# A fused attention and feed-forward kernel on one core: the written-out order of batches 2 to 7 is planned anew with longer planned DMA times

## The chip, the core and the metric

The kernel runs on one core of one Trainium2 chip. A core has a matrix engine (TensorE, PE in the profile), a vector engine (VectorE, DVE), a scalar engine (ScalarE, ACT), a general engine (GpSimd, POOL) and a sync engine (SP) that computes nothing and issues DMAs. Each engine works through its own list of instructions in order and stops at the first one whose inputs are not ready. DMAs are issued by SP, ACT or POOL and run beside the engines. The metric is the device time of one execution in microseconds (us); the median of several runs is compared.

## The reference

```python
scores = scale * np.matmul(q, k_all.transpose(0, 1, 3, 2))   # k_all: 16 beacon rows, then k
scores = np.where(causal, -1000000000.0, scores)             # the beacon columns are never masked
scores = scores - scores.max(-1, keepdims=True)
a = np.exp(scores)
a /= a.sum(-1, keepdims=True) + 1e-09
attn = np.matmul(a, v_all)
x = attn.transpose(0, 2, 1, 3).reshape(B * S, H * D)
h = x @ w_in
g = np.where(h > 0.0, h, np.exp(np.minimum(h, 0.0)) - 1.0)
out = g @ w_out
```

There are 8 batches of 8 heads, 576 tokens and 64 elements a head. `x` has 4608 rows of 512; `w_in` is 512 x 2048, `w_out` 2048 x 512. Inputs and output are float32, the products run on 16-bit types.

## The kernel before

**Attention** is done by pairs of heads, four pairs to a batch; pair 13 is the second pair of batch 3. For each pair the scores are made transposed (keys on the partitions) in two steps, `do_SC` on units (0, 1) and then on units (2, 3). Each step fills both PSUM buffers called `sc`; ScalarE takes the exponential of one unit at a time (`do_exp`) and so frees one buffer, and GpSimd zeroes the masked triangle (`do_mask`). Then the product with v follows (`do_AV`, line 473) in two pieces, (0,) with 6 matmuls and (1, 2) with 24, and VectorE divides by the sum of the row (`do_norm`).

**The feed-forward part** runs on 11 tiles of rows (three small ones and eight of 512). For each 512-row tile, 16 steps `do_mm1` (M1, line 529, four matmuls each) are followed by the exponential on ScalarE (`do_e`, line 536), a clamp on GpSimd (`do_clamp`, line 540) and a join on VectorE (`do_join`, line 549) that leaves the 16-bit activation `gt`. Then come 16 quarters `do_mm2` (M2, line 563, four matmuls each), four to a block of 128 rows, a copy out of PSUM (`do_osb`) and a store. M1 5,13 is step 13 of tile 5; M2 5,0,3 is the last quarter of the first row block of tile 5. M1, M2 and AV share four PSUM buffers called `ff`. A buffer of M1 comes back after the join, one of AV after the division.

**Loads.** In batches 0 to 2 k and q are turned by TensorE. From batch 3 (`PE_B = 3`) each batch has five loads of k (issued by SP), five of q (ACT) and five of v, all in runs of 256 bytes; a cast to bfloat16 on DVE or POOL (`cast_tok`, line 346; the strings `TOK` say which, "0" is DVE, first three letters k, last three q); and ten transposing DMAs from SP (`turn_tok`, line 353). From batch 2 the finished x rows are also turned by DMA from SP (`turn_x`, line 359, five to a batch); the first M1 of a tile waits for them.

**The order is written out by a planner.** `Plan` holds every piece of work with an engine, a sort key, a planned duration, its dependencies and the buffers that it takes and gives. `Plan.run` plays the plan through, engine by engine, smallest key first among what is ready, and emits the instructions in the order that comes out. A planned duration is nothing but a number in this play: it changes no transfer, only the order. DMAs are pieces of work on one planned "DMA" engine. The keys come from `place(b, a)`, which is `32 * (b - 1) + 8 * a + SHIFT[b]` for batch b, and from `PACES` and `LAG` for the feed-forward tiles.

When the instructions are emitted, the DMAs of SP and ACT together get eight completion semaphores in turn, and each DMA also waits until the one eight places before it has landed.

Of the kernel before, what the change touches and what calls it, by code (L numbers as in the profile page):

```python
# [138 lines left out]
def kernel(  # L139
# [122 lines left out]
    with tc.tile_pool(name="psum", bufs=1, space=bass.MemoryType.PSUM) as psum:  # L262
# [15 lines left out]
        add = plan.add  # L278
# [295 lines left out]

        SHIFT = [-8.8, -12.16, 3.82, 4.72, 5.51, 10.18, 13.79, 3.06]
        AT = [-49.72, -1.57, -0.78, 0.0, 0.42, 1.22, 1.53, -12.56]
        AT0 = [[-47.18, -49.17, -39.96, -41.23], [-43.3, -38.3, -37.64, -35.42], [-44.55, -19.83, -27.66, -35.41]]
        PACES = [(-18.35, 2.5, 7.99, 12.09), (-6.14, 3.4, 55.13, 1.74), (-8.68, 1.33, 24.3, 1.89), (37.46, 1.31, 15.04, 2.29), (66.83, 1.23, 21.13, 2.7), (104.32, 2.11, 33.83, 1.91)]  # L580
        W_AFTER = [[-52.45, -48.57, -122.34, -273.93], [16.05, 17.94, 11.68, 32.16]]
        DMA_AT = [-282.17, -172.71, 307.5]
        TOK = ("011110", "111001", "110011", "011001", "101101")
        ON_POOL = "11110000"
        X_ON_ACT = "00"
        LAG = 10.75
        URGE = -104.22
        Q_ON_ACT = "01101011"
        FIRST = (
            "q2 v0 k2 q1 v6 v9 k1 q3 k3 b1 v8 q6 q4 v1 q5 v7 v3 v2 k4 q7 k5 v5 v4 k7 k6 ").split()  # L590
        ON_ACT = "01"
        V_ON_ACT = "10011111"

        def place(b, a):
            return 32 * (b - 1) + 8 * a + SHIFT[b]

# [32 lines left out]
        def plan_v(b):  # L629
            for jc in range(NKC):  # L630
                key = load_key(f"v{NKC * b + jc}", place(b - 1, 1.8 + 0.4 * jc))
                on, eng = QUEUES[V_ON_ACT[b] == "1"]
                got = load(key, 1.22 if b < 3 else 1.3, partial(load_v, b, jc, eng), take=["vst"], issue=1.2 if jc == 0 else 0.6, units=8, on=on,
                           deps=v_issue[b - 1] if b > 1 else ())
                v_issue.setdefault(b, []).append(issues[on][-1])
                v_cast[b, jc] = add(
                    "DVE", place(b, -0.7 + 0.16 * jc), 0.56, partial(cast_v, b, jc),
                    deps=[got] + last_AV.get(b - 2, []), give=["vst"])
# [7 lines left out]
        turned, last_SC, turns, readers = {}, {}, [], {}  # L646
# [3 lines left out]
        def plan_tok(b):  # L650
            turned[b] = []
            for is_k in (True, False):
                for c in range(0, NKC, 2):
                    m = min(2, NKC - c)
                    i = (0 if is_k else 0.5) + c // 2
                    on, eng = QUEUES[ON_ACT[not is_k] == "1"]
                    gots = [load(place(b, 0) - 30 + i + 0.01 * j, 1.3, partial(load_tok, b, is_k, c + j, eng), units=8, on=on,
                                 take=["st"] if j == 0 else [], issue=1.2 if is_k and c + j == 0 else 0.65) for j in range(m)]
                    on_dve = TOK[b - PE_B][3 * (not is_k) + c // 2] == "0"
                    cast = add("DVE" if on_dve else "POOL", place(b, DMA_AT[0]) + i, 0.36 * m if on_dve else 0.53 * m,  # L660
                               partial(cast_tok, b, is_k, c, m, nc.vector if on_dve else nc.gpsimd),
                               deps=gots, take=["sb"], give=["st"])
                    for j in range(m):
                        s = add("SP", place(b, DMA_AT[1]) + i, 1.25, partial(turn_tok, b, is_k, c + j),
                                deps=[cast] + last_SC.get(b - 2, []), take=ring4)
                        turned[b].append(add("DMA", place(b, DMA_AT[1]) + i, 0.65, None, deps=[s],
                                             give=ring4 + (["sb"] if j == m - 1 else []), lat=1.0, parts=8))

        def plan_T2(n, key):
# [28 lines left out]
        def plan_pair(n):  # L698
            b, hp = divmod(n, HP)
            at = lambda a: place(b, hp + a)  # L700
            key = AT0[0][hp] - 4 if b == 0 else at(AT[1])
            ready = plan_T2(n, key) if b == 0 else plan_T(n, key) if b < PE_B else turned[b]
            masked = {}
            SC = None
            steps = [((0,), AT0[0][hp]), ((1, 2), AT0[1][hp]), ((3,), AT0[2][hp])] if b == 0 else \
                [((0, 1), at(AT[2])), ((2, 3), at(AT[3]))]
            for units, key in steps:
                SC = add(
                    "PE", key, sum(0.00024 * 2 * CUT.width[u] + 0.02 for u in units), partial(do_SC, n, units),
                    deps=ready + [SC], take=["sc"] * len(units), mode=1, lat=0.19)  # L710
                last_kq[n] = SC
                last_SC.setdefault(b, []).append(SC)
                first_SC.setdefault(n, SC)
                for u in units:
                    w = CUT.width[u]
                    x = add("ACT", key + 0.16, 0.14 + 0.00166 * w, partial(do_exp, n, u), deps=[SC],
                            take=["et"], give=["sc"])
                    masked[u] = [x]
                    for jc, q0, w in CUT.units[u]:
                        dw = min(w, P * jc + P - NB - q0, kc_sz[jc])  # L720
                        if dw > 0:
                            masked[u].append(add(
                                "POOL", key + 0.8, 0.2 + 0.0008 * 2 * dw, partial(do_mask, n, u, jc, q0, dw), deps=[x]))
                            if b < 2:
                                marks.append(masked[u][-1])
            normed = []
            for r, groups in enumerate([(0,), (1,), (2,)] if b == 0 else [(0,), (1, 2)]):
                key = AT0[r][hp] + 2.4 if b == 0 else at(AT[4 + r])
                us = [u for g in groups for u in CUT.of_range[g]]
                blks = blocks_of(groups)  # L730
                AV = add(
                    "PE", key, 0.0304 * 2 * sum(BLOCKS[i][2] for i in blks), partial(do_AV, n, groups),
                    deps=[o for u in us for o in masked[u]] + [v_cast[b, jc] for jc in range(BLOCKS[blks[-1]][2])],
                    take=["ff", "av"], give=["et"] * len(us), mode=0, lat=0.19)
                last_AV.setdefault(b, []).append(AV)
                normed.append(add(
                    "DVE", key - URGE, 0.32 + 0.148 * len(blks), partial(do_norm, n, groups),
                    deps=[AV, last_xT.get(n - 2 * HP)] + last_X.get(b - 2, []), give=["ff", "av"]))
                if b >= XB:
                    for blk in blks:  # L740
                        part.setdefault(blk, []).append(normed[-1])
                    if hp == HP - 1:
                        for blk in blks:
                            s = add("SP", at(AT[7]), 1.25, partial(turn_x, b, blk), deps=part.pop(blk), take=ring4)
                            turns.append((b, s))
                            done = add("DMA", at(AT[7]), 0.65, None, deps=[s], give=ring4, lat=1.0, parts=8)
                            last_X.setdefault(b, []).append(done)
                            for g, (lo, hi) in enumerate(CUT.ranges):
                                if lo <= BLOCKS[blk][0] < hi:
                                    scaled.update({(b * HP + p, g): done for p in range(HP)})  # L750
                    continue
                if b and r == 0:
                    continue
                if b:
                    groups, key = (0, 1, 2), at(AT[6])
                blks = blocks_of(groups)
                X = last_xT[n] = add(
                    "PE", key, sum(0.0025 + BLOCKS[i][1] / 2400 for i in blks) + 0.02, partial(do_xT, n, groups),
                    deps=normed, take=["ff"], mode=0, lat=0.19)
                w = sum(BLOCKS[i][1] for i in blks)  # L760
                normed = []
                on_act = X_ON_ACT[b] == "1"
                done = add("ACT" if on_act else "DVE", key - URGE, 0.17 + 0.00104 * w if on_act else 0.15 + w / 1920,
                           partial(do_xcopy, n, groups, nc.scalar if on_act else nc.vector), deps=[X], give=["ff"])
                for g in groups:
                    scaled[n, g] = done
# [107 lines left out]
```

## Time and profile before

| what | value |
|---|---|
| median of 3 runs | 361.16 us (360.14 to 361.88) |
| the profiled execution | 358.78 us |
| its span, first to last instruction | 356.9 us |
| PE busy | 344.9 us (97%) |
| DVE, ACT, POOL busy | 57%, 55%, 52% |
| granted TensorE clock | 1.0 of full speed |

The page of the profile gives the busy time of each engine; "the waits" list who was idle for whom; "the timeline" lists instructions in order of time, merged where equal ones follow each other, and in brackets the idle time of the engine before it and the engine or DMA that ended it. "ACTq" and "SPq" rows are DMAs being issued. "xN" at the end of a row is the number of instructions.

### The profile page before, as it was taken

What the parts mean: (1) busy time and instruction counts of PE and PEld (TensorE: products, weight loads), DVE (VectorE), ACT (ScalarE), POOL (GpSimd) and SP (SyncE); (2) the same over time, 40 slices, a digit from 0 to 9 for tenths busy, and PEclk for the clock granted to TensorE, in tenths of its full rate; (3) what the DMA queues carried; (4) which work ended last, traced back from release to release, by engine and by line L of the source; (5) the groups of instructions that cost most, each with busy time, mean ns of one, the idle gap of its engine ahead of it and who ended that gap; (6) DMA issues with size and microseconds to landing.
All of it is one profiled execution on the core that took longest, in us unless ns stands there. A gap on an engine that the chain in (4) does not pass through costs nothing.

```text
span 356.9 us, 8475 instructions
## 1 busy us (share of the span) xinstructions
PE 344.9 (97%) x3299; PEld 195.0 (55%) x3299; DVE 204.6 (57%) x421; ACT 194.6 (55%) x289; POOL 185.3 (52%) x360
## 2 busy tenths in 40 slices
PE   8998999999998999999999999999999999999996
PEld 5667887545454445545576664555555444444444
DVE  1477797565763647556856565566555545554321
ACT  2576887567554656675666547657664243433200
POOL 5487776557733664567557546555453344334200
PEclk9999999999999999999999999999999999999999
DMA  7999995799999978899999799997301311000022
GB/s 204 256 283 229 195 240 106 222 212 153 165 217 148 201 149 178 146 232 172 167 209 166 174 152 190 182 183 143 69 31 44 83 53 37 29 29 32 29 83 95
DMA packets 139480, 52.55 MB, mean 147 GB/s; under 512 B 127536, under 2 KB 131888, under 8 KB 139440
## 3 DMA queue, kind: packets, MB, share of 16 engines
q1 hardware_dynamic: 82640, 34.34, 45.7%
q10 hardware_dynamic: 52576, 13.47, 21.3%
q0 software_dynamic: 4224, 4.19, 7.0%
q8 instruction: 26, 0.43, 0.5%
q14 instruction: 14, 0.11, 0.1%
HBM read 37.22 MB, written 9.44 MB: 131 GB/s over the span
## 4 chain that ended last, share of the span: by engine, by line
PE 83%; DMA 7%; DVE 3%; POOL 3%; issue 1%; ACT 1%; SPq 1%; ACTq 0%; POOLq 0%
PE hps L529 33%; PE ops L563 33%; PE av L473 7%; PE sc L439 7%; DMA w_in<-in_moe_w_in_dram 3%; DMA st<-in_k_dram 2%; POOL et L454 2%; PE spare L274 2%; DMA kT<-st 1%; DVE gt L549 1%; DMA st<-in_beacon_k_dram 1%; ACT et L448 1%; PE tr L388 1%; POOL e L540 1%; DVE x L489 0%
## 5 line engine op out<-in xcount | busy, mean ns | idle before, releaser
L529 PE MATMUL hps<-xT,w_in 128*128 128x512 f16 (+2 forms) x768 | 141.5, 326 | 3.3 <-DMA w_in<-in_moe_w_in_dram 1.2
L563 PE MATMUL ops<-w_out,gt 128*128 128x512 f16 (+1 forms) x592 | 143.9, 374 | 0.0
L549 DVE SCALAR_TENSOR_TENSOR gt<-e,hps 128x512 f16<-128x512 f32 x144 | 97.4, 684 | 69.9 <-POOL e L540 69.6
L540 POOL TENSOR_SCALAR e<-e 128x512 f32<-128x512 f32 x144 | 89.1, 621 | 89.6 <-ACT e L536 87.6
L536 ACT ACTIVATE e<-hps 128x512 f32<-128x512 f32 x144 | 85.7, 600 | 86.7 <-PE hps L529 79.2
L448 ACT ACTIVATE et<-sc 128x768 f16<-128x768 f32 (+3 forms) x128 | 104.4, 863 | 38.4 <-PE sc L439 35.3
L529 PEld LDWEIGHTS <-w_in 128*128 128x128 f16 x768 | 67.0, 98 | 56.5 <-issue 3.4
L454 POOL TENSOR_SCALAR_AFFINE_SELECT et<-et 128x256 f16<-128x256 f16 (+2 forms) x160 | 62.0, 412 | 46.5 <-ACT et L448 43.5
L563 PEld LDWEIGHTS <-gt 128*128 128x128 f16 x592 | 54.2, 98 | 55.9 <-issue 1.7
L473 PEld LDWEIGHTS <-et 128*128 128x128 f16 (+1 forms) x960 | 36.5, 97 | 15.4 <-issue 4.1
L569 DVE COPY osb<-ops 128x512 f32<-128x512 f32 (+1 forms) x37 | 25.0, 675 | 34.4 <-PE ops L563 34.3
L473 PE MATMUL av<-v,et 128*128 128x65 f16 (+1 forms) x960 | 40.2, 193 | 2.7 <-POOL et L454 1.4
L439 PE MATMUL sc<-qT,kT 64*128 64x80 bf16 (+3 forms) x704 | 35.0, 228 | 0.0
L489 DVE TENSOR_TENSOR x<-av,rl 128x256 f16<-128x256 f32 (+2 forms) x68 | 32.0, 471 | 2.3
L439 PEld LDWEIGHTS <-kT 64*128 64x128 bf16 x704 | 20.6, 95 | 20.9 <-issue 19.3
L488 DVE RECIPROCAL rl<-av 128x4 f32<-128x4 f32 (+2 forms) x68 | 12.4, 182 | 23.5 <-PE av L473 23.1
L373 DVE CAST v<-vst 128x512 f16<-128x512 f32 (+1 forms) x40 | 21.5, 543 | 4.0 <-DMA vst<-in_v_dram 3.8
L274 PE MATMUL spare<-ones 128*128 128x256 bf16 x115 | 20.4, 300 | 1.7 <-DVE ones L812 1.3
L346 POOL CAST st<-st 128x1024 bf16<-128x1024 f32 (+2 forms) x19 | 16.2, 854 | 6.3 <-DMA st<-in_k_dram 3.4
L274 PEld LDWEIGHTS <-ones 128*128 128x128 bf16 x115 | 11.1, 107 | 6.7 <-issue 2.3
L323 POOL CAST st<-st 128x1152 bf16<-128x1152 f32 x8 | 9.1, 1142 | 5.7 <-DMA st<-in_q_dram 3.8
L346 DVE CAST st<-st 128x1024 bf16<-128x1024 f32 (+2 forms) x11 | 8.4, 762 | 1.6 <-DMA st<-in_q_dram 0.8
(35 smaller groups left out, 67.6 us busy)
## 6 DMA issues: line engine op xcount, KB each, us to landing
out_dram<-osb SPq DMA_DIRECT2D x35, 256.0 KB, 2.7
st<-in_q_dram ACTq DMA_DIRECT2D x20, 256.0 KB, 4.4
vst<-in_v_dram ACTq DMA_DIRECT2D x18, 256.0 KB, 4.5
st<-in_k_dram SPq DMA_DIRECT2D x15, 256.0 KB, 4.9
st<-in_k_dram SPq DMA_DIRECT2D x12, 288.0 KB, 7.2
st<-in_q_dram SPq DMA_DIRECT2D x11, 288.0 KB, 6.9
w_in<-in_moe_w_in_dram POOLq DMA_DIRECT2D x4, 512.0 KB, 14.2
w_out<-in_moe_w_out_dram POOLq DMA_DIRECT2D x4, 512.0 KB, 20.1
```

The costliest lines, as they stand in the source:

```text
L274: nc.tensor.matmul(out=spare[:, 0:2 * P], lhsT=ones[:, 0:P], rhs=ones, start=True, stop=True)
L439: nc.tensor.matmul(out=sc[:, h, o:o + w], lhsT=kT[D * h:D * h + D, P * jc:P * jc + P], rhs=qT[D * h:D * h + D, q0:q0 + w], start=True, sto ...
L448: nc.scalar.activation(out=et[:, :, 0:w], in_=scs[n, u][:, :, 0:w], func=AFT.Exp, bias=0.0, scale=float(1.0 / (D ** 0.5)))
L454: nc.gpsimd.affine_select(out=et[:, :, c0:c0 + dw], in_=et[:, :, c0:c0 + dw], compare_op=ALU.is_ge, fill=fill0, base=q0 + NB - P * jc, pat ...
L473: nc.tensor.matmul(out=av[:, c:c + D + 1], lhsT=ets[n, CUT.unit_of[jc, at]][0:m, h, col:col + P], rhs=v16[0:m, jc, 2 * hp + h, 0:D + 1], s ...
L489: nc.vector.tensor_tensor(out=x16s[b % 2][:, blks[0]:blks[0] + nb, P * hp:P * hp + P].rearrange("q i (h d) -> q i h d", d=D), in0=av[:, :, ...
L529: nc.tensor.matmul(out=hps[:, o:o + z - a], lhsT=w_in16[:, cc, P * fc:P * fc + P], rhs=xT[cc][:, a % RING:a % RING + z - a], start=(cc == ...
L536: nc.scalar.activation(out=e, in_=hpss[tt, i], func=AFT.Exp, bias=0.0, scale=1.0)
L540: nc.gpsimd.tensor_scalar(out=e, in0=e, scalar1=1.0, scalar2=0.0, op0=ALU.min, op1=ALU.max)
L549: nc.vector.scalar_tensor_tensor(out=gt, in0=es[tt, i], scalar=1.0, in1=hpss[tt, i], op0=ALU.subtract, op1=ALU.max)
L563: nc.tensor.matmul(out=opss[tt, t4][:, cols], lhsT=gts[tt, fc][:, P * t4:P * (t4 + 1)], rhs=w_out16[:, fc, cols], start=(fc == 0), stop=(f ...
L569: nc.vector.tensor_copy(out=osb[:, slice(*cols)], in_=opss[tt, t4][:, slice(*cols)])
```

## The change

Planned durations: a load of 256-byte runs goes from 1.3 to 1.45 us for k and q of batches 3 to 7 and for v of those batches, and a transposing DMA from 0.65 to 0.75 us. The keys of the later batches, the two last own paces of the feed-forward tiles and the offset of those behind (`LAG`) are other numbers. `TOK` moves casts: 18 of the 30 casts of batches 3 to 7 are on DVE, where there were 11. The last letter of `V_ON_ACT` lets SP and not ACT issue the v loads of batch 7. Nothing else differs; the same matmuls, activations and DMAs are emitted, in another order.

```diff
-        SHIFT = [-8.8, -12.16, 3.82, 4.72, 5.51, 10.18, 13.79, 3.06]
+        SHIFT = [-8.8, -12.16, 3.82, 7.68, 7.37, 15.72, 15.25, 20.7]
...
-        PACES = [(-18.35, 2.5, 7.99, 12.09), (-6.14, 3.4, 55.13, 1.74), (-8.68, 1.33, 24.3, 1.89), (37.46, 1.31, 15.04, 2.29), (66.83, 1.23, 21.13, 2.7), (104.32, 2.11, 33.83, 1.91)]
+        PACES = [(-18.35, 2.5, 7.99, 12.09), (-6.14, 3.4, 55.13, 1.74), (-8.68, 1.33, 24.3, 1.89), (37.46, 1.31, 15.04, 2.29), (75.69, 1.42, 8.27, 3.74), (111.87, 2.41, 34.18, 1.87)]
...
-        DMA_AT = [-282.17, -172.71, 307.5]
-        TOK = ("011110", "111001", "110011", "011001", "101101")
+        DMA_AT = [-284.54, -157.9, 350.32]
+        TOK = ("001110", "110000", "010101", "111000", "001000")
...
-        LAG = 10.75
+        LAG = 17.42
...
-        V_ON_ACT = "10011111"
+        V_ON_ACT = "10011110"
...
-                got = load(key, 1.22 if b < 3 else 1.3, partial(load_v, b, jc, eng), take=["vst"], issue=1.2 if jc == 0 else 0.6, units=8, on=on,
+                got = load(key, 1.22 if b < 3 else 1.45, partial(load_v, b, jc, eng), take=["vst"], issue=1.2 if jc == 0 else 0.6, units=8, on=on,
...
-                    gots = [load(place(b, 0) - 30 + i + 0.01 * j, 1.3, partial(load_tok, b, is_k, c + j, eng), units=8, on=on,
+                    gots = [load(place(b, 0) - 30 + i + 0.01 * j, 1.45, partial(load_tok, b, is_k, c + j, eng), units=8, on=on,
...
-                        turned[b].append(add("DMA", place(b, DMA_AT[1]) + i, 0.65, None, deps=[s],
+                        turned[b].append(add("DMA", place(b, DMA_AT[1]) + i, 0.75, None, deps=[s],
...
-                            done = add("DMA", at(AT[7]), 0.65, None, deps=[s], give=ring4, lat=1.0, parts=8)
+                            done = add("DMA", at(AT[7]), 0.75, None, deps=[s], give=ring4, lat=1.0, parts=8)
```

## The prediction

> **What bounds the kernel now.** I read the page's head first, then PE's waits, the busy time by stretches, the timeline around each gap of PE, and last the groups and the DMA issues.
>
> ```profile
> span 356.9 us, 8475 instructions
> PE 344.9 (97%) x3299; PEld 195.0 (55%) x3299; DVE 204.6 (57%) x421; ACT 194.6 (55%) x289; POOL 185.3 (52%) x360
> ...
> PE av L473 <- POOL et L454: 1.4, 1, 1.4
> PE av L473 <- DVE gt L549: 1.1, 2, 0.6
> PE hps L529 <- DVE gt L549: 0.9, 2, 0.7
> PE hps L529 <- DVE x L489: 0.8, 1, 0.8
> PE hps L529 <- DVE v L373: 0.3, 1, 0.3
> ...
> 86.00:257.00 171.00, 166.17 (x1676) 90.52 (x1675) 103.04 (x205) 105.29 (x153) 96.98 (x190) 1.00 0.97 173
> ```
>
> TensorE is the bound, at the full clock. The orders of the two kernels on PE agree up to 86 us of the trace; in the stretch from there to 257 us PE is busy for 166.2 of 171 us (the first two numbers of the last row), idle for 4.8, and the five waits of PE shown, all of them in that stretch, sum to 4.5 us. The same matmuls are issued before and after, with the same number of changes between scores and other products, so nothing but these 4.5 us can be won there. After 257 us PE has none of these waits, though the last AVs still stand there, and from about 280 us on there is feed-forward work alone.
>
> ```profile
> 332.66 20.92 PE L563 MATMUL ops<-w_out,gt 128*128 128x512 f16 x112
> ```
>
> Before, this last run of M2 has no M1 in it; after, 18 quarters of M2 (15.6 us) stand behind the last M1, so the end stays as it is: nothing there is counted.
>
> Below, a "distance" is PE's own work between two points of the written order, by these rows: 0.86 us for four matmuls of M1 or M2, 0.49 for a score step of 8 matmuls (108.00 to 108.49), 0.74 for an AV of 24, and the same for the others.
>
> ```profile
> 95.15 0.34 PE L473 MATMUL av<-v,et 128*128 128x65 f16 x6 [0.58 <-DVE gt L549]
> ...
> 105.72 0.52 PE L439 MATMUL sc<-qT,kT 64*128 64x256 bf16 x14
> ...
> 108.00 0.55 PE L439 MATMUL sc<-qT,kT 64*128 64x240 bf16 x8
> 108.49 0.91 PE L473 MATMUL av<-v,et 128*128 128x65 f16 x24
> 109.23 1.02 PE L563 MATMUL ops<-w_out,gt 128*128 128x512 f16 x4
> 111.61 0.62 PE L473 MATMUL av<-v,et 128*128 128x65 f16 x6 [1.36 <-POOL et L454]
> ...
> 104.02 3.46 SPq L359 DMA_TRANSPOSE xT<-x  x2
> 109.83 0.37 ACTq L340 DMA_DIRECT2D st<-in_q_dram  x1
> 110.33 1.70 ACT L448 ACTIVATE et<-sc 128x736 f16<-128x736 f32 x2 [2.63 <-DMA xT<-x]
> 111.18 0.74 POOL L454 TENSOR_SCALAR_AFFINE_SELECT et<-et 128x224 f16<-128x224 f16 x2 [3.09 <-ACT et L448]
> ```
>
> **Where the longest gap comes from.** The 1.36 us at 111.61 begin on ACT: it must issue a q load before the next exponentials, and that load waits, as the eighth DMA after it, for the first transpose of x, issued by SP at 104.02. ACT stands for 2.63 us, so the mask comes late and so does AV. The planner does not know this wait. The same happens at 131.77:
>
> ```profile
> 131.77 0.39 ACTq L369 DMA_DIRECT2D vst<-in_v_dram  x1
> 132.26 1.08 ACT L536 ACTIVATE e<-hps 128x512 f32<-128x512 f32 x2 [2.70 <-PE sc L439]
> ```
>
> After this stop of ACT a join is late and AV waits 0.53 us (part of the 1.1 above).
>
> **The change, part by part.**
>
> *Planned durations, keys, paces.* No transfer gets longer; the order changes. Summed up in PE's work, the first scores of batches 3 to 7 move from 79.2, 115.3, 146.0, 183.6, 216.0 us to 81.0, 114.2, 150.2, 189.5, 229.8, and the last AV from 249.4 to 257.1: the same DMAs get 3% more time. All seven gaps stand in places that are laid anew, so I take all of them away: -4.5. What comes in their place:
>
> ```profile
> 160.97 0.55 PE L439 MATMUL sc<-qT,kT 64*128 64x240 bf16 x8
> 161.41 0.78 ACT L448 ACTIVATE et<-sc 128x736 f16<-128x736 f32 x1 [0.46 <-PE sc L439]
> 162.09 1.02 ACT L448 ACTIVATE et<-sc 128x1024 f16<-128x1024 f32 x1
> ...
> L448 ACT ACTIVATE et<-sc 128x800 f16<-128x800 f32 x22 | 18.4, 836 | 0.0
> L448 ACT ACTIVATE et<-sc 128x768 f16<-128x768 f32 x22 | 17.8, 810 | 13.5 <-PE sc L439 13.4
> ```
>
> (a) Score steps drawn together. The next step needs both `sc` buffers. They are free 0.44 + 0.81 + 0.84 + 0.1 = 2.2 us after the start of a step on units (2, 3), and the second buffer is first needed 0.25 us into the next step: 1.95 us. After, scores (2, 3) of pair 12 and (0, 1) of pair 13 have 1.61 us between them: 0.35 us of idle PE (0 to 0.7, since the 0.1 for the signal and the 0.25 are estimates from the spacing of these rows). AV of pair 11 comes 0.27 too early for its mask by the same rows.
>
> (b) The end of tile 4. From the start of an M1 to its join:
>
> ```profile
> 206.86 1.03 PE L529 MATMUL hps<-xT,w_in 128*128 128x256 f16 x8
> 207.93 0.60 ACT L536 ACTIVATE e<-hps 128x512 f32<-128x512 f32 x1 [1.32 <-PE hps L529]
> 208.62 0.61 POOL L540 TENSOR_SCALAR e<-e 128x512 f32<-128x512 f32 x1 [1.30 <-ACT e L536]
> 209.41 0.68 DVE L549 SCALAR_TENSOR_TENSOR gt<-e,hps 128x512 f16<-128x512 f32 x1
> ```
>
> 209.41 + 0.68 - 206.86 = 3.2 us. After, M1 4,11 to 4,15 and two AVs want four `ff` buffers of which M2 holds one, and ACT has 7 e of 0.6, two exponentials and three DMA issues of 0.4, in all 7 us of work in 7 us. Followed step by step, M1 4,13, M2 4,0,2 and two AVs each come 0.1 to 0.3 early: 0.5 (0 to 1.0).
>
> (c) ACT stopped by the eighth DMA before. I counted, in both orders, ACT's loads from v of batch 3 on whose DMA eight places before stands less than 4.6 us of PE work earlier; the landings are
>
> ```profile
> vst<-in_v_dram ACTq DMA_DIRECT2D x18, 256.0 KB, 4.5
> xT<-x SPq DMA_TRANSPOSE x30, 2.9
> kT<-st SPq DMA_TRANSPOSE x25, 3.7
> ```
>
> There are ten before and eight after, so the waits do not go; other ones come. The worst after is the third v load of batch 5: 1.7 us behind the transpose that it waits for, which takes 3.7, so ACT is held some 1.3 to 2 us between e of M1 5,12 and 5,13; M2 5,0,3 needs the join of 5,15 and has no reserve: 1.3 (0 to 2.7). The other seven have M2 to cover them.
>
> (d) First M1 of a tile behind `turn_x`. Now M1 of tiles 7 and 8 wait for transposes of x (the 0.3 and 0.8 of the waits; at 213.02 PE's weight load shows it as `xT`).
>
> ```profile
> 213.02 0.98 PEld L529 LDWEIGHTS <-w_in 128*128 128x128 f16 x6 [0.82 <-DMA xT<-x]
> ...
> 252.09 1.02 PE L529 MATMUL hps<-xT,w_in 128*128 128x512 f16 x4 [0.84 <-DVE x L489]
> ```
>
> The distance from the last transpose needed to the M1 was 2.2, 3.0 and 8.5 us for tiles 7, 8 and 9 and becomes 3.3, 3.3 and 2.5; with 2.9 to land and an SP that is late now and then I put 0.3, 0.3, 0.4: 1.0 (0 to 2.5).
>
> (e) Pairs 28 to 31. Between 234.4 and 245.4 us of PE's work ACT has the exponentials of five score steps (three of 1.65 us, two of 1.80) and four e of 0.6: 10.9 us in 11.0. A late one has no room to catch up: 0.5 (0 to 1.2).
>
> *Seven casts from POOL to DVE.*
>
> ```profile
> L346 POOL CAST st<-st 128x1024 bf16<-128x1024 f32 x11 | 11.4, 1036 | 3.7 <-DMA st<-in_k_dram 3.4 <-issue 0.3
> L346 DVE CAST st<-st 128x1024 bf16<-128x1024 f32 x9 | 6.3, 702 | 1.6 <-DMA st<-in_q_dram 0.8 <-DMA st<-in_k_dram 0.7
> L346 POOL CAST st<-st 64x512 bf16<-64x512 f32 x4 | 2.4, 602 | 2.6 <-DMA kT<-st 2.6
> L346 DVE CAST st<-st 80x512 bf16<-80x512 f32 x1 | 1.0, 958 | 0.0
> ...
> 93.40 1.11 DVE L346 CAST st<-st 64x512 bf16<-64x512 f32 x1
> ```
>
> Three full and four small casts: DVE gets 3 x 0.70 + 4 x 1.03 = 6.2 us more, POOL 5.5 us less; both are about 60% busy in the stretch, so most of it is covered by idle time. But a small cast of half the elements takes longer on DVE than a full one (1.11 and 0.96 against 0.70 us), and the one at 93.40 stood before the joins for which AV at 95.15 waited 0.58 us and the M1 behind it 0.26 (part of the 0.9 of the waits): 0.84 us with 11 casts on DVE. For 18 casts I take 0.84 x 18 / 11 = 1.4 (0.4 to 2.2).
>
> [...]
>
> *The v loads of batch 7 on SP.* Six issues of about 0.4 us leave ACT, 2.4 us, and no ACT stop in batch 7 is left; the gain is in (e). What queues behind them on SP are stores, which have a spare buffer, and transposes of x, in (d).
>
> **The sum.** -4.5 + 0.35 + 0.27 + 0.5 + 1.3 + 1.0 + 0.5 + 1.4 = +0.8. The profiled execution goes from 358.8 to 359.6; the median of the runs lies 2.4 above the profiled one, so 361.2 becomes 362.0. About 0.5% (1.8 us) is what a measurement of this kernel can tell from no change, so this forecast is "no change". With every new term at its low end the sum is -4.1, at its high end about +6.
>
> **The rivals.**
>
> *The drawn-out transfers do what they are for.* The DMAs get more time, ACT's loads find the eighth DMA before landed, transposes of x come in time; only (a), (b), (e) and 0.4 of the casts stay: -4.5 + 2.0 = -2.5, 358.7 us. For it: eight short distances and not ten, and distances before tiles 4 to 8 that grow by 0.3 to 1.7 us. Against it: 1.7 us in batch 5, and 2.5 before tile 9.
>
> *ACT becomes the bound in the attention runs.* Before, three of the distances from score step to score step leave less than 0.4 us over what the exponentials need; after it is eleven. Where a DMA issue of 0.4 us or a held one stands between, PE waits at once. At 0.4 us for each of the eleven this is 4.4 in place of (a) and (e), 1.1: +4.1, 365.3 us. It decides once ACT is more than about 0.2 us late in most of these runs. Against it: in the trace of before, score steps at the same short distance (105.72 to 108.00) made no gap.
>
> [...]
>
> **How the numbers follow.** No change, 0.43, its own range 360.2 to 363.0; faster 0.21; ACT as the bound 0.24; DVE and POOL 0.12. Slower by over 0.5% is the sum of the last two, 0.36. The range 358.6 to 365.6 reaches to the three rivals' times and leaves the far ends of the unknown terms out.
>
> **What would show it.** Right: PE's idle time in the stretch with attention stays at 4 to 6 us, with other instructions ending it; a gap before M2 5,0,3 after an ACT stop at a v load; L529 waiting for `xT` at the first M1 of tiles 7, 8 or 9. [...] A PE busy time that differs from 344.9 by over 1 us would upset the ground of the whole sum.

## The result: faster, and outside the range

| | before | after |
|---|---|---|
| median of 6 runs | 360.65 us (359.03 to 362.71) | 355.56 us (354.51 to 357.65) |
| the profiled execution | 358.78 us | 354.51 us |
| its span | 356.9 us | 352.8 us |

The ratio is 0.986, with a 95% interval of 0.9816 to 0.9904: the change saves 3.5 to 6.6 us. The forecast was 362.0 us, its range 358.6 to 365.6; the time lies 3 us below the lower end, and on the side of the first rival (358.7 us).

The profile's head and TensorE's waits (in each row: the sum in us, how often, the longest), kernel after:

```profile
span 352.8 us, 8449 instructions
PE 344.7 (98%) x3299; PEld 195.6 (55%) x3299; DVE 206.1 (58%) x428; ACT 193.6 (55%) x289; POOL 180.3 (51%) x353
...
PE sc L439 <- ACT et L448: 0.8, 2, 0.4
...
PE hps L529 <- DVE gt L549: 0.4, 1, 0.4
PE hps L529 <- DMA xT<-x: 0.4, 1, 0.4
PE ops L563 <- DVE gt L549: 0.2, 1, 0.2
```

TensorE's work is what it was, 344.7 us against 344.9, so the ground of the forecast's sum holds: only idle time can be won. None of the old waits of AV is left. (The waits left out lie in the first 86 us.) The busy time by stretches, kernel after (length, then PE, PEld, DVE, ACT, POOL busy, granted clock, DMA share, GB/s):

```profile
0.00:86.00 86.00, 83.25 (x1068) 58.32 (x1069) 55.36 (x143) 57.05 (x85) 57.31 (x116) 1.00 1.00 213
86.00:261.00 175.00, 172.84 (x1660) 93.56 (x1659) 107.12 (x212) 104.17 (x154) 93.08 (x184) 1.00 0.93 170
```

Between 86 and 261 us PE is idle for 2.2 of 175 us; before, it was idle for 4.8 us from 86 to 257, and for as much from 86 to 261. The timeline has the gaps one by one; in brackets the idle time before the row:

```profile
106.15 0.39 PE L439 MATMUL sc<-qT,kT 64*128 64x256 bf16 x4 [0.39 <-ACT et L448]
126.75 1.02 PE L529 MATMUL hps<-xT,w_in 128*128 128x512 f16 x4 [0.44 <-DVE gt L549]
147.84 0.39 PE L439 MATMUL sc<-qT,kT 64*128 64x256 bf16 x4 [0.39 <-ACT et L448]
175.80 0.39 PE L563 MATMUL ops<-w_out,gt 128*128 128x512 f16 x1 [0.21 <-DVE gt L549]
244.48 1.90 PE L529 MATMUL hps<-xT,w_in 128*128 128x512 f16 x8 [0.43 <-DMA xT<-x]
```

Counted along the written order these are the second half of scores (0, 1) of pair 13, M1 4,9, scores (0, 1) of pair 18, M2 5,0,3, and M1 8,0. They sum to 1.9 us; the seven gaps of before summed to 4.6.

### The profile page after: what moved, and what is told of

Its sections match the earlier page's. It is cut to its first block, busy times and chain, and to the rows that moved or that the text cites. A ratio compares the mean times of both kernels' runs of the same rounds, so it can differ in the third digit from the quotient of the medians.

```text
span 352.8 us, 8449 instructions
## 1 busy us (share of the span) xinstructions
PE 344.7 (98%) x3299; PEld 195.6 (55%) x3299; DVE 206.1 (58%) x428; ACT 193.6 (55%) x289; POOL 180.3 (51%) x353
## 4 chain that ended last, share of the span: by engine, by line
PE 82%; DMA 8%; DVE 2%; POOL 2%; ACT 2%; SPq 2%; issue 1%; ACTq 0%; DVEq 0%; POOLq 0%
PE ops L563 31%; PE hps L529 30%; PE av L473 8%; PE sc L439 7%; DMA st<-in_k_dram 3%; PE spare L274 3%; DMA xT<-x 3%; DMA kT<-st 2%; DVE gt L549 1%; PE tr L388 1%; ACT et L448 1%; ACT e L536 1%; POOL e L540 1%; PE xt L499 1%; POOL et L454 1%
## 5 line engine op out<-in xcount | busy, mean ns | idle before, releaser
L529 PEld LDWEIGHTS <-w_in 128*128 128x128 f16 x768 | 67.9, 98 | 56.5 <-issue 3.0
L439 PEld LDWEIGHTS <-kT 64*128 64x128 bf16 x704 | 20.7, 95 | 19.9 <-issue 18.1
L346 DVE CAST st<-st 128x1024 bf16<-128x1024 f32 (+2 forms) x18 | 11.4, 643 | 2.1 <-DMA st<-in_k_dram 1.0
L346 POOL CAST st<-st 128x1024 bf16<-128x1024 f32 (+2 forms) x12 | 10.7, 892 | 3.2 <-DMA st<-in_k_dram 2.8
```

What stands on the lines that cost most here:

```text
L439: nc.tensor.matmul(out=sc[:, h, o:o + w], lhsT=kT[D * h:D * h + D, P * jc:P * jc + P], rhs=qT[D * h:D * h + D, q0:q0 + w], start=True, sto ...
L529: nc.tensor.matmul(out=hps[:, o:o + z - a], lhsT=w_in16[:, cc, P * fc:P * fc + P], rhs=xT[cc][:, a % RING:a % RING + z - a], start=(cc == ...
```

## How much of it is the order, and how much the execution

On PE the first 86 us are the same work in the same order, and yet they differ: PE is busy for 83.25 us of them after and was for 82.18 before, so some 1.1 us of the profiled difference has nothing to do with the change. To keep this apart I took a second profile of each kernel and cut each at the start of the 69th instruction that ACT executes, which stands ahead of all that the change moves. (The first of the 69 loads a table; the expectations below call the 69th an activation.)

For the second profile of the kernel before: 

> The kernel before once more, for a second profile of it. If the spread between executions comes from the first 86 us, which all these orders share, the time up to the same instruction (72.6 us in the first profile) differs by 1 us or more and PE's idle time behind it stays near 4.5 us. If it comes from the later part, that idle time differs by 1 us or more.

For the second profile of the kernel after:

> The kernel after, unchanged, for a second profile of it. If the gain is one of the order, TensorE's gaps behind the first 86 us are again 1.9 to 2.9 us in sum, and the stretch from the 69th activation on ACT to the end is again 280 to 282.5 us against 284.3 and 285.1 in the two profiles of the kernel before. If the profile after was only a lucky one, the stretch is over 283.5 us and the gaps over 4 us.

| profile | time | start of ACT's 69th instruction | from there to the end | PE's gaps in that part |
|---|---|---|---|---|
| before | 358.78 | 72.60 | 284.25 | 4.6 |
| before, second | 358.52 | 71.61 | 285.07 | 5.1 |
| after | 354.51 | 71.67 | 281.13 | 1.9 |
| after, second | 354.82 | 71.65 | 281.45 | 2.6 |

The difference repeats. Of the means, 4.0 us apart, 3.4 lie behind the cut, and 2.6 of these are gaps that the timeline shows; 0.45 lie ahead of the cut and 0.2 outside the span. The 0.75 us that are left behind the cut stand in no gap of 0.15 us or more. Most of them are an effect of how gaps are counted. A gap begins at the listed end of the last matmul, but in a running stream the next matmul starts before that end: four matmuls of M1 are listed with 1.02 us and follow each other every 0.86. So a gap costs about 0.16 us more than its number. Behind the cut there are 7 and 9 gaps before and 5 and 5 after, three fewer in the mean: an estimate of 0.5 us. The remaining 0.25 us have no cause that I know.

The medians are 5.1 us apart, with 3.5 as the near end of the interval, so 3.4 to 4.0 us of profiles is at its edge; the last section has a possible reason for the rest.

The gaps of the second profile of after (one of 0.40 us before M1 3,11 left out):

```profile
...
106.82 0.40 PE L439 MATMUL sc<-qT,kT 64*128 64x256 bf16 x4 [0.39 <-ACT et L448]
131.82 1.89 PE L529 MATMUL hps<-xT,w_in 128*128 128x512 f16 x8 [0.94 <-DVE gt L549]
138.24 0.90 PE L473 MATMUL av<-v,et 128*128 128x65 f16 x24 [0.25 <-DVE x L489]
244.78 1.90 PE L529 MATMUL hps<-xT,w_in 128*128 128x512 f16 x8 [0.63 <-DMA xT<-x]
```

Pair 13 and M1 8,0 are there in both and repeat to 0.2 us; the others, M1 4,9, pair 18 and M2 5,0,3 in the first and M1 3,11, M1 4,12 and the AV of pair 15 in the second, come and go.

Two of them have a cause that the prediction did not have: a cast that stands at the head of its engine before its DMA has landed, with clamps or joins queued behind it. The timeline of the first profile before M1 4,9, and of the second before M1 4,12:

```profile
124.36 1.04 POOL L346 CAST st<-st 128x1024 bf16<-128x1024 f32 x1 [1.91 <-DMA st<-in_k_dram]
...
125.36 1.76 POOL L540 TENSOR_SCALAR e<-e 128x512 f32<-128x512 f32 x3
```

```profile
130.53 0.64 DVE L346 CAST st<-st 64x512 bf16<-64x512 f32 x1 [1.61 <-DMA kT<-st]
...
131.10 1.27 DVE L549 SCALAR_TENSOR_TENSOR gt<-e,hps 128x512 f16<-128x512 f32 x2
```

The 0.40 us before M1 3,11 in the second profile is of the same kind: a cast of k on DVE starts at 86.38, after a wait of 1.26 us for its load, and two joins stand behind it.

## The experiments

**Longer planned durations alone.** The old places, paces and casts, with the four new durations:

```diff
# against the kernel before
-                got = load(key, 1.22 if b < 3 else 1.3, partial(load_v, b, jc, eng), take=["vst"], ...
+                got = load(key, 1.22 if b < 3 else 1.45, partial(load_v, b, jc, eng), take=["vst"], ...
-                    gots = [load(place(b, 0) - 30 + i + 0.01 * j, 1.3, partial(load_tok, b, is_k, c + j, eng), ...
+                    gots = [load(place(b, 0) - 30 + i + 0.01 * j, 1.45, partial(load_tok, b, is_k, c + j, eng), ...
-                        turned[b].append(add("DMA", place(b, DMA_AT[1]) + i, 0.65, None, deps=[s],
+                        turned[b].append(add("DMA", place(b, DMA_AT[1]) + i, 0.75, None, deps=[s],
-                            done = add("DMA", at(AT[7]), 0.65, None, deps=[s], give=ring4, lat=1.0, parts=8)
+                            done = add("DMA", at(AT[7]), 0.75, None, deps=[s], give=ring4, lat=1.0, parts=8)
```

> The kernel before with the longer planned DMA times alone (1.45 and 0.75 us), every key, pace, cast and queue as before. Theory A (later places for the DMA-bound work are what helps): the first scores of batches 3 to 7 move to 81.0, 115.1, 151.0, 185.2 and 220.4 us of PE's work, and the distances from the transposes of x to the first M1 of tiles 4 to 8 grow from 2.2 to 3.0 us to 3.1 to 4.7, so most of the gain of 5 us shows: 356 to 358 us. Theory B (the casts on DVE and the batch 7 loads on SP are what helps): nothing of it is here, 360 to 361 us. Theory C (any other order loses some amount, the keys have to fit): the score steps are drawn together without room (the rows of before give 1.4 us of forced idle), 361 to 365 us.

Measured: 359.95 us, ratio 0.998 (0.9944 to 1.0015): no change. In this profile ACT is stopped for less (1.5 us by DMAs, against 4.7 and 3.4 in the two profiles of before), and the gap of 1.36 us at the first AV piece of pair 13 is gone; its second piece waits 0.54 us as before. But a later tile pays. The timeline of this kernel:

```profile
252.08 1.90 PE L529 MATMUL hps<-xT,w_in 128*128 128x512 f16 x8 [2.43 <-DMA xT<-x]
```

M1 8,0 stands 2.43 us for its turned x, where before it stood 0.84. So here ACT is stopped for less, and with the old places most of the time comes back as one late transpose. It is not a general effect of the longer durations: with the new places, ACT's waits for DMAs sum to 3.7 and 4.7 us in the two profiles of after.

**The new places with the old durations.** The kernel after, the four durations put back:

```diff
# against the kernel after
-                got = load(key, 1.22 if b < 3 else 1.45, partial(load_v, b, jc, eng), take=["vst"], ...
+                got = load(key, 1.22 if b < 3 else 1.3, partial(load_v, b, jc, eng), take=["vst"], ...
...
-                            done = add("DMA", at(AT[7]), 0.75, None, deps=[s], give=ring4, lat=1.0, parts=8)
+                            done = add("DMA", at(AT[7]), 0.65, None, deps=[s], give=ring4, lat=1.0, parts=8)
```

> The changed kernel with the old planned DMA times (1.3 and 0.65 us); keys, paces, casts and queue changed. Theory A: the later batches move back (first scores at 81.8, 110.9, 145.9, 179.3, 216.1), ten DMAs of ACT stand less than 4.6 us behind the eighth before, so the waits of PE come back to 4 to 6 us after 86 us: 359 to 362 us. Theory B: casts and queue are as in the changed kernel, 355 to 357 us. Theory C: 358 to 364 us.

Measured: 361.31 us, ratio 1.0063 (1.0022 to 1.0103): slightly slower than before. The longest of ACT's waits for a DMA and of PE's waits, and the longest gap with what POOL did ahead of it:

```profile
ACT et L448 <- DMA st<-in_q_dram: 4.2, 2, 2.2
...
PE hps L529 <- DVE gt L549: 2.9, 4, 1.7
...
159.41 1.04 POOL L346 CAST st<-st 128x1024 bf16<-128x1024 f32 x1 [2.57 <-DMA st<-in_k_dram]
160.42 1.77 POOL L540 TENSOR_SCALAR e<-e 128x512 f32<-128x512 f32 x3
...
161.81 1.02 PE L529 MATMUL hps<-xT,w_in 128*128 128x512 f16 x4 [1.73 <-DVE gt L549]
```

With a planned length that is too short, the planner lets POOL take the cast of a k load that has not landed. POOL stands there for 2.57 us, three clamps queue behind the cast, the joins are late, and M1 5,6 waits 1.73 us. Here one sees what the planned duration does: it moves no transfer, but it decides how far behind its load a cast stands in the list of its engine. The longer durations do not end such stops: in the two profiles of after the longest are 1.91 and 1.61 us, in the rows before M1 4,9 and 4,12 above.

Both halves alone gain nothing, and together they save 1.4%. My step "no transfer gets longer; the order changes" was true, and I then took the durations for a small matter; they are what the places were drawn for.

**Are the casts or the v loads of batch 7 in it?** Each undone alone in the kernel after:

```diff
# casts as before
-        TOK = ("001110", "110000", "010101", "111000", "001000")
+        TOK = ("011110", "111001", "110011", "011001", "101101")
...
# in another kernel: v loads of batch 7 by ACT again
-        V_ON_ACT = "10011110"
+        V_ON_ACT = "10011111"
```

> The changed kernel with the casts on the engines of before (11 of 30 on DVE, not 18). PE's order is nearly that of the changed kernel. Theory A: no change beyond 1 us, 355 to 357 us. Theory B (POOL was held by casts that wait for their loads): waits of PE behind masks and clamps come back, 358 to 361 us. My prediction's term for the casts: 0.6 us faster than the changed kernel.

> The changed kernel with the five v loads of batch 7 issued by ACT again. Theory A and B: a stop of ACT of 1 to 3 us at one of these loads (one stands 1.6 us behind the eighth DMA before), at most 1 us of it on PE: 355 to 357 us. If the queue is what helps: 357 to 360 us.

Measured: 355.37 us, ratio 0.9866 (0.9782 to 0.9949), and 355.92 us, ratio 0.9868 (0.9799 to 0.9937). Neither differs from after's 0.986; with four executions each, though, the intervals are 1.7% and 1.4% wide, so that the 1.4 us of the prediction's term (0.4%) could hide in them. The gaps tell more: behind 86 us they sum to 2.3 and 2.6 us in these two profiles, and to 1.9 and 2.6 in the two of after. The casts on DVE by their shape, first two rows of the kernel after, then one of that with the casts of before (busy us, mean ns, idle time before them):

```profile
L346 DVE CAST st<-st 128x1024 bf16<-128x1024 f32 x12 | 8.8, 736 | 1.1 <-DMA st<-in_k_dram 1.0
L346 DVE CAST st<-st 64x512 bf16<-64x512 f32 x4 | 1.9, 476 | 1.0 <-DMA kT<-st 1.0
```

```profile
L346 DVE CAST st<-st 128x1024 bf16<-128x1024 f32 x9 | 6.4, 708 | 0.0
```

With 18 casts on DVE a full one takes 736 ns in the mean, with 11 it takes 708; the small ones take 476 and 452. The 4.2 us that DVE gets more lie, for the most part, beside other work. What a cast on DVE can cost is its wait, the last numbers of the rows.

**The places and the paces, each undone alone** in the kernel after:

```diff
# places
-        SHIFT = [-8.8, -12.16, 3.82, 7.68, 7.37, 15.72, 15.25, 20.7]
+        SHIFT = [-8.8, -12.16, 3.82, 4.72, 5.51, 10.18, 13.79, 3.06]
...
# in another kernel: paces and LAG
-        PACES = [..., (75.69, 1.42, 8.27, 3.74), (111.87, 2.41, 34.18, 1.87)]
+        PACES = [..., (66.83, 1.23, 21.13, 2.7), (104.32, 2.11, 33.83, 1.91)]
-        LAG = 17.42
+        LAG = 10.75
```

> The changed kernel with the places of the batches as before (SHIFT alone undone; durations, paces, casts and queue changed). The last AV then stands at 243.3 us of PE's work and not at 257.1, and twelve, not eight, loads of ACT stand less than 4.6 us behind the eighth DMA before. Theory A' (the later places are the part that gives the DMAs room): the gain goes, 358 to 361 us. Rival (the paces of the feed-forward tiles, laid to the longer planned times, are that part): 355 to 357 us.

> The changed kernel with the paces of the feed-forward tiles 4 and later as before (PACES and LAG undone; durations, places, casts and queue changed). The distance from the transposes of x to the first M1 of tiles 5, 8 and 9 falls to 2.5, 2.3 and 1.7 us, below the 2.9 us that they take to land. Theory A': half of the gain or more stays, 356 to 358 us. Rival (the paces): the gain goes, 359 to 362 us, with PE's waits at M1 for the transposes of x or for joins.

Measured: with the old places 364.59 us, ratio 1.0139 (1.0063 to 1.0216), with the old paces 357.86 us, ratio 0.9954 (0.992 to 0.9989). Without the new places the gain is gone and more, beyond both expectations; the paces carry about 0.9 of the 1.4%, so that a third of the gain stays, which lies between the two theories. (The keys of casts and transposes, `DMA_AT`, were not undone alone.) The largest gap with the old places, the DMA issues ahead of it, and the granted clock behind it:

```profile
239.02 0.63 ACTq L340 DMA_DIRECT2D st<-in_q_dram  x1
242.60 0.86 DVE L346 CAST st<-st 128x1024 bf16<-128x1024 f32 x1 [0.26 <-DMA st<-in_q_dram]
243.49 2.50 SPq L353 DMA_TRANSPOSE qT<-st  x2
247.37 0.61 PE L439 MATMUL sc<-qT,kT 64*128 64x256 bf16 x4 [4.66 <-DMA qT<-st]
```

```profile
248.00:250.00 2.00, 2.00 (x5) 0.66 (x6) 0.00 (x0) 1.02 (x1) 0.00 (x0) 0.50 0.24 42
250.00:252.00 2.00, 2.00 (x17) 1.15 (x16) 0.00 (x0) 0.45 (x1) 0.00 (x0) 0.50 0.57 114
252.00:254.00 2.00, 2.00 (x34) 1.42 (x32) 1.09 (x3) 0.85 (x2) 0.61 (x1) 0.76 0.74 197
```

The first scores of batch 7 (pair 28) want the turned q; a q load issued at 239.02 is cast at 242.60 and turned from 243.49 on, and with the old place of batch 7 (3.06 in `SHIFT`, 20.7 in the new) PE comes to it 4.66 us too early. With the new places the key of batch 7 is 17.6 later, over half of the 32 from batch to batch, so more of the feed-forward steps stand ahead of it: summed up in PE's work, the last AV is at 257.1 us and not at 243.3. That is the room for its loads, casts and transposes. The 4.66 us and the half clock behind them are most of what this kernel loses.

**ACT without its loads.** If ACT's stops at loads are what costs, let SP issue them, in the plan of before:

```diff
# against the kernel before
-                got = load(key, 1.22 if b < 3 else 1.3, partial(load_v, b, jc, eng), ...
+                got = load(key, 1.22 if b < 3 else 1.3, partial(load_v, b, jc, eng if b < 4 else nc.sync), ...
-                    gots = [load(place(b, 0) - 30 + i + 0.01 * j, 1.3, partial(load_tok, b, is_k, c + j, eng), ...
+                    gots = [load(place(b, 0) - 30 + i + 0.01 * j, 1.3, partial(load_tok, b, is_k, c + j, nc.sync), ...
```

> The kernel before in its own order, but all loads of q from batch 3 on and of v from batch 4 on are issued by SP at the same places, so that no wait for the eighth DMA before stands on ACT behind 90 us. If the stops of ACT cost what the prediction read from the trace (1.36 and 0.53 us on PE), those two gaps go and it is 1 to 2 us faster than before: 358 to 359 us. Rival: SP, which also issues the transposes, now waits in ACT's place and the transposes come later: same as before or up to 3 us slower, 360 to 363 us.

Measured: 366.33 us, ratio 1.0138 (1.0065 to 1.0211), longer than both expectations. ACT is stopped by no DMA any more, and the AV of pair 13 does not wait, in the same written order. The waits moved to SP, where the same DMAs wait for the one eight places before and hold the transposes behind them. The waits, the longest gap, and the clock behind it:

```profile
PE hps L529 <- DMA xT<-x: 6.4, 3, 3.0
DVE v L373 <- DMA vst<-in_v_dram: 13.4, 11, 2.8
...
116.72 11.68 PE L529 MATMUL hps<-xT,w_in 128*128 128x512 f16 x40 [2.98 <-DMA xT<-x]
```

```profile
118.00:120.00 2.00, 2.00 (x6) 0.69 (x5) 0.04 (x1) 0.60 (x1) 0.61 (x1) 0.50 1.09 256
...
122.00:124.00 2.00, 2.00 (x10) 0.80 (x8) 0.98 (x2) 1.19 (x2) 0.67 (x2) 0.85 1.15 253
```

This settles that the long gap of before came from ACT's stop, as the prediction had it; it also shows that here the stops cost more on SP than on ACT: M1 waits 6.4 us for transposes of x, where the prediction had put 1.36 and 0.53 us of gaps down to ACT's stops.

**Longer still.** If more planned length is good in itself, still more should not hurt. The kernel after with 1.6 in place of 1.45, and 0.85 in place of 0.75:

```diff
# against the kernel after
-                got = load(key, 1.22 if b < 3 else 1.45, partial(load_v, b, jc, eng), ...
+                got = load(key, 1.22 if b < 3 else 1.6, partial(load_v, b, jc, eng), ...
...
-                            done = add("DMA", at(AT[7]), 0.75, None, deps=[s], give=ring4, lat=1.0, parts=8)
+                            done = add("DMA", at(AT[7]), 0.85, None, deps=[s], give=ring4, lat=1.0, parts=8)
```

> The kernel after with the planned lengths of the drawn-out loads raised once more, from 1.45 to 1.6, and of the turns from 0.75 to 0.85, its places and paces unchanged. Theory that the places and paces were fitted to 1.45 and 0.75: the planner, running later with its transfers, puts elements of the score, M1 and M2 chains past their drawn places, as it did when the old places met the new lengths or the new places the old lengths; 358 to 363 us, TensorE's idle time behind the first 86 us at 4 us or more against 1.9 after. Theory that longer planned transfers are worth something whatever the places: 354 to 356.5 us, TensorE's waits for turned x and for ACT's stopped exps no longer than after's 0.4 us.

Measured: 362.54 us, ratio 1.0067 (1.0033 to 1.0101). The profiled execution took 367.0 us, 4.5 above the median, so its lines are read for the place of the gaps and not for their sum; the last section says where most of the 4.5 us come from. The timeline around its longest gap, and the clock there:

```profile
261.51 1.18 SPq L353 DMA_TRANSPOSE kT<-st  x1
264.23 1.18 SPq L353 DMA_TRANSPOSE qT<-st  x1
265.46 3.14 SPq L369 DMA_DIRECT2D vst<-in_v_dram  x4
269.06 0.43 DVE L373 CAST v<-vst 128x512 f16<-128x512 f32 x1 [4.53 <-DMA vst<-in_v_dram]
269.54 0.25 PE L473 MATMUL av<-v,et 128*128 128x65 f16 x3 [2.17 <-DVE v L373]
```

```profile
270.00:272.00 2.00, 2.00 (x7) 0.73 (x5) 1.54 (x5) 0.60 (x1) 0.18 (x1) 0.52 1.07 244
272.00:274.00 2.00, 2.00 (x12) 0.60 (x11) 1.35 (x3) 0.68 (x1) 0.43 (x1) 0.63 0.01 3
```

The v loads of batch 7 come out last on SP, behind transposes, and the first AV of batch 7 (pair 28) stops in its middle. In the kernel after they are the last on SP too, but the load that this AV needs is issued at 253.56, 8.2 us ahead of it; here it is issued at 265.46, 1.65 us ahead. So 1.45 and 0.75 are not simply "more": the places fit that length, and with 1.3 as with 1.6 they fit no longer. That a third set of places, drawn for 1.6, would do better or worse was not tried.

No run was better than the kernel after by more than the intervals tell.

## Why the prediction was wrong

Its first step held: PE's busy time did not move, six of the seven gaps went, and the one before M1 8,0 is smaller (0.43 and 0.63 for 0.84). (The -4.5 for the old gaps was a little small: with 0.16 us more for each of the seven they were worth 5.7.) The new gaps were to be 5.3 us (the sum of its terms without -4.5) and were 1.9 and 2.6. Term by term:

| term | predicted | first profile of after | second | verdict |
|---|---|---|---|---|
| (a) scores of pair 13 | 0.35 | 0.39 | 0.39 | right |
| (a) AV of pair 11 | 0.27 | 0 | 0 | wrong, small |
| (b) end of tile 4, buffers | 0.5 | 0 | at most 0.25, at an AV of pair 15 | too large |
| (c) M2 5,0,3 behind ACT's stop | 1.3 | 0.21 | 0 | place right, size wrong |
| (d) tiles 7, 8, 9 | 0.3, 0.3, 0.4 | 0, 0.43, 0 | 0, 0.63, 0 | one of three |
| (e) pairs 28 to 31 | 0.5 | 0 | 0 | wrong |
| seven casts to DVE, by their length | 1.4 | 0 | at most 0.5 | wrong |
| not forecast: casts that wait for a DMA | none | 0.44, at M1 4,9 | 0.40 and 0.94, at M1 3,11 and 4,12 | missed |
| not forecast: scores of pair 18 | none | 0.39 | 0 | missed |

The "at most 0.5" is a part of the 0.40 and 0.94 below it and no gap of its own. The steps that failed are (c), (e) and the casts, 3.2 us of the sum, of which 0.2 to 0.5 came. In tile 4 there were gaps of about the forecast size, 0.44 and 0.94 us for 0.5, but that is luck: they come from the casts that wait, and not from the four `ff` buffers of (b).

*(c).* "M2 5,0,3 needs the join of 5,15 and has no reserve." The stop came, where it was foretold. The timeline of after:

```profile
168.20 2.54 PE L529 MATMUL hps<-xT,w_in 128*128 128x512 f16 x11
171.33 0.40 ACTq L369 DMA_DIRECT2D vst<-in_v_dram  x1
171.43 1.03 PE L529 MATMUL hps<-xT,w_in 128*128 128x512 f16 x4
171.83 0.60 ACT L536 ACTIVATE e<-hps 128x512 f32<-128x512 f32 x1 [2.19 <-DMA kT<-st]
172.32 1.08 ACT L536 ACTIVATE e<-hps 128x512 f32<-128x512 f32 x2
172.50 1.77 POOL L540 TENSOR_SCALAR e<-e 128x512 f32<-128x512 f32 x3 [2.17 <-ACT e L536]
...
173.76 0.79 DVE L373 CAST v<-vst 128x512 f16<-128x512 f32 x1
...
174.47 1.27 DVE L549 SCALAR_TENSOR_TENSOR gt<-e,hps 128x512 f16<-128x512 f32 x2
```

M1 5,15 starts at 171.43 and its last reader, M2 5,0,3, would have stood at 175.80 - 0.21 = 175.59: 4.16 us, against the 3.2 of the chain from M1 to join that the prediction itself had worked out. There was a reserve of 0.95 us. And the stop of 2.19 us did not reach the join whole: e of 5,13 is 1.9 us late (171.83, its M1 was through at about 169.9), but the three e behind the stop run one after the other, and M1 5,15 comes later in any case, behind M2 5,0,0. Its clamp ends at 174.27, about 0.5 late by the rows of (b), where a clamp ends 2.4 us after the start of its M1. Another 0.6 come on DVE, where a cast of v (173.76) and the join of 5,14 stand ahead, so that the join of 5,15 ends at 175.74, 1.1 later than 171.43 + 3.2. 1.1 - 0.95 is the 0.2 seen. I had carried the stop over to the end undiminished.

*The casts.* The 0.84 us in the trace of before that I put down to one small cast on DVE, and scaled by 18/11, was a cost of the old order, not of casts as such: with all casts as before, the new order has gaps of the same sum (2.3 us against 1.9 and 2.6). Scaling a gap that one instruction shares with its neighbours by the number of such instructions was the mistake. The small casts of 1.11 and 0.96 us, from which this term was built, take 0.48 and 0.42 us in the mean in the new order, and all 18 take 643 ns. The chance of 0.12 for DVE and POOL stood for a loss at each of the 18 casts; no run shows such a loss. In the second profile the two casts ahead of the gaps took 0.99 and 0.64 us, 0.5 us together above the usual 0.68 and 0.42, and why they did is not shown. What did make joins late there is the wait for a DMA (1.26 and 1.61 us), and a cast on POOL can do the same, as the 0.44 us before M1 4,9 show.

*(e) and the second rival.* ACT was not the bound: two gaps before scores of 0.39 us each in the first profile and one of 0.39 in the second, where the rival had 0.4 us at each of eleven. The distances were as short as I had counted them, but ACT was not late when it came to them.

*The weighing.* I counted distances in the order and saw ten short ones become eight, which looked like no change. The count was the wrong reading: what matters is which of them stand on PE's path, and before two of ten did (at 111.61 and 134.33), after one of eight did, for 0.2 us, and in the first profile only. The distances before tiles 4 to 8, which grew by 0.3 to 1.7 us, told more, and they were in the text, as what speaks for the first rival. That rival's own terms, (a), (b), (e) and 0.4 of the casts, came to +2.0, and the two profiles have 1.9 and 2.6, but the agreement is luck: of its terms only the 0.35 of (a) came in both. Nor did its mechanism hold as a whole. Transposes of x came in better time (the waits before M1 7,0 and 8,0 fell from 1.2 and 1.5 us in the two profiles of before to 0.4 and 0.6), but ACT's loads did not find the eighth DMA before landed: ACT waits for DMAs for 4.7 and 3.4 us before and 3.7 and 4.7 us after. The stops stayed and stand where PE has a reserve.

*The base.* "The median lies 2.4 above the profiled one" was the smaller error: with 6 runs it is 1.9 for before, and 1.1 for after. By the profiles alone the right sum, -4.6 + 1.9, gives 356.1 us for the profiled execution, which took 354.5; of the 1.6 us between, 1.1 is the shared first part and what lies around the span, and 0.4 is in no listed gap; with 0.16 us for each of the two gaps fewer, 0.3 of it is accounted for.

## What to carry to other kernels

Where an order is planned, a planned duration and the planned places are one setting: try them together, since each alone can look worthless or harmful (0.998 and 1.006 here, 0.986 together). A stop on an engine off the path is worth what is left of it at the instruction that PE waits for (0.21 us of ACT's 2.19 here): work the reserve out from the row of that reader, and let a queue that runs back to back make up lost time, before charging the stop whole. Look up what stood ahead of each gap before booking it under a term: a gap of the right size in the right tile had another cause here. And cut the profile where the shared part ends: in the first pair of profiles 1 us of 4 would have been taken for the change.

## What was not expected of the hardware

In some gaps of PE, or right behind them, the granted clock fell to 0.50, and such a gap cost more than its own length. With the loads issued by SP, the gap of 2.98 us was followed by 40 matmuls in 11.68 us; the same 40 in the kernel before:

```profile
115.22 8.80 PE L529 MATMUL hps<-xT,w_in 128*128 128x512 f16 x40
```

So that gap cost 2.9 us once more (clock 0.94, 0.50, 0.50, 0.50 and 0.85 in the five times 2 us from 114 on, which is 6.8 us at 0.50). With the old places the gap of 4.66 us was of the same kind (clock 0.53, 0.50, 0.50 and 0.76 in the four times 2 us from 246 on, again 6.8 us at 0.50). The length alone does not tell whether it happens. The stretches around the gap of 2.43 us with the longer durations alone, and around the other long gap of the kernel with the loads on SP (2.81 us, at 222.94), keep the clock at 1.00. In the profiled execution with the still longer durations, it was 0.50 for 3.4 us at each of three gaps: two of 2.17 us (one in the first 86 us, which have 0.98 in the mean, and the one at 269.54) and one of 1.40 us (at 142.34, with 0.95, 0.50 and 0.70 in the three times 2 us from 142 on). The three together cost an estimated 5 us at half the clock. The mean clock of that execution is 0.986, that of seven of the ten others 0.995; by this difference alone an estimated 3.3 of the 4.5 us that it lies above its median come from the clock. The two stretches that kept the clock:

```profile
252.00:254.00 2.00, 1.92 (x10) 0.79 (x12) 0.00 (x0) 0.60 (x1) 0.16 (x1) 1.00 0.55 106
```

```profile
224.00:226.00 2.00, 2.00 (x22) 0.98 (x21) 0.66 (x1) 1.72 (x3) 1.05 (x2) 1.00 1.18 295
```

By these rows and those further up, the clock was halved for 3.4 us at a time (still longer durations) or for 6.8 us (loads on SP, old places). What decides whether a gap halves it, these runs do not show.

Neither kernel of the comparison has a gap at half the clock in its profiles: the mean granted clock is 1.0 and 0.999 in the two of before, 1.0 in both of after. The 0.001 of 357 us is an estimated 0.4 us, in one profile of the four, so the clock does not explain the 4.0 us between them. For the medians this is not shown. One stretch of 3.4 us at half the clock lowers the mean clock of an execution of 357 us to an estimated 0.995, and 11 of 45 later executions of before had a mean clock of 0.990 to 0.995; their median time is 362.1 us, that of the other 34 is 359.4. The six executions of after had 0.999 to 1.0; of the six of before only the profiled one has its clock on record.
